# Routed attention and a gated feed-forward block: 32x32 block transposes on VectorE, and a reciprocal by log, exp and a Newton step

## The chip, the cores and the metric

The kernel runs on one core of a Trainium2 chip. The metric is the device time of one execution in microseconds; a comparison takes the median of several executions. The core's engines run side by side, each working through its own list of instructions in order: TensorE (PE; its weight loads are listed as PEld), VectorE (DVE), ScalarE (ACT), GpSimd (POOL), and SyncE (SP), which here only issues transfers. They wait for each other through semaphores. TensorE writes its results to PSUM; everything else lies in SBUF.

## The reference, cut to what matters

There are 4 batches of 8 heads, 768 positions and 64 values per head. Each query and each key is assigned to one of 16 clusters by the largest similarity with a centroid, a query attends only to keys of its own cluster, and the result goes through a feed-forward block with a smooth gate.

```python
def _attn_ref(q, k, v, centroids):            # q, k, v: (4, 8, 768, 64), centroids: (8, 16, 64)
    ...                                       # q_n, k_n, c_n: q, k, centroids divided by their norms
    q_assign = np.argmax(np.einsum('bhsd,hcd->bhsc', q_n, c_n), axis=-1)
    k_assign = np.argmax(np.einsum('bhsd,hcd->bhsc', k_n, c_n), axis=-1)
    mask = q_assign[:, :, :, None] == k_assign[:, :, None, :]
    scores = scale * np.matmul(q, k.transpose(0, 1, 3, 2))
    scores = np.where(mask, scores, -1000000000.0)
    scores = scores - np.max(scores, axis=-1, keepdims=True)
    attn = np.exp(scores)
    attn = attn / (np.sum(attn, axis=-1, keepdims=True) + 1e-09)
    return np.matmul(attn, v)

def _moe_ref(x, w_in, w_out):                 # x: (3072, 512), w_in: (512, 2048), w_out: (2048, 512)
    h = x @ w_in
    sp = np.maximum(h, 0.0) + np.log1p(np.exp(-np.abs(h)))
    g = h * erf(sp)
    return g @ w_out
```

## The kernel before

The 32 heads are worked off as 16 pairs, four pairs to a batch. For each pair the kernel runs `route` (cluster of each query and key, written as masks), `shift` (whether a query finds any key of its cluster, which sets the shift of its scores), then 12 units of `scores` and two of `attend`, one for each half of the queries. `route` and `shift` of the next pair run beside the units of this one, in small portions. The feed-forward block of a batch is a stream of matmuls that is portioned out between the units of the next batch; for the last batch it runs by itself at the end. During the first pairs the kernel also converts the weights, which come as 64-bit floats and are put together from their two 32-bit words by VectorE.

The masks: `qm` and `km` hold, for one head in one half of the partitions, the one-hot cluster (for q multiplied by minus 2 to the 60th, for k inverted), and in the other half a bf16 copy of the other head's q or k. Their product is added to the scores and drives those of foreign clusters far down.

```python
    aq = const.tile([P, HJ, 2, 2, D], BF16, name="aq")
    ak = const.tile([P, HJ, 2, 2, D], BF16, name="ak")
    ...
    def load(p, nm, src, pl):
        ...
        t = pl.tile([P, NJ, 2, D], F32, name="in_" + nm)
        for e in range(2):
            nc.sync.dma_start(out=t[:, :, e], in_=src[b, h0 + e].rearrange("(p j) d -> p j d", p=P))
    ...
    def convert(dst, src):                     # one of 16 pieces of the weights
        ...                                    # load, ACT Square, then seven VectorE steps of 128x1024
        nc.vector.scalar_tensor_tensor(
            out=m, in0=m, scalar=0x40000000, in1=x, op0=ALU.bitwise_xor, op1=ALU.bitwise_and
        )
        ...
    def route(p):
        st = pairs[p]
        for nm in "qk":
            raw = rowp.tile([P, S], F32, name=nm + "T")
            low = rowp.tile([P, 2, S], BF16, name=nm + "m")
            for half in range(2):
                pt = ps_t.tile([P, HJ, P], F32, name="pt", tag="t")
                for jj in range(HJ):
                    nc.tensor.transpose(out=pt[:, jj], in_=st[nm][:, HJ * half + jj]..., identity=ident)
                ...                            # ACT: q copied with the factor D**-0.5, k copied, into raw
                for e in range(2):
                    nc.gpsimd.tensor_copy(out=low[(1 - e) * D : (2 - e) * D, e, ...], in_=raw[...])
                yield
            ...
        load_qk(p + 1)
        psim = ps_t.tile([P, HW], F32, name="psim", tag="t")
        for g in range(4):
            nc.tensor.matmul(psim[2 * C * g : 2 * C * (g + 1)], lhsT=ccT[:, p % HP], ...)
        sims = routep.tile([P, HW], F32, name="sims")
        nc.scalar.copy(out=sims, in_=psim)
        yield
        pt = ps_t.tile([P, HJ, P], F32, name="pt", tag="t")
        for jj in range(HJ):
            nc.tensor.transpose(out=pt[:, jj], in_=sims[:, jj * P : (jj + 1) * P], identity=ident)
        ...                                    # VectorE: mx, the maximum, and its place; GpSimd: times rank;
                                               # VectorE: mr, the maximum of that; aq, ak, the one-hot masks
        for nm, src in (("qm", aq), ("km", ak)):
            pb = ps_t.tile([P, NJ, P], BF16, name="pb", tag="t")
            for j in range(NJ):
                nc.tensor.transpose(out=pb[:, j], in_=src[:, j % HJ, j // HJ]..., identity=identb)
            for e in range(2):
                ...                            # qm: VectorE, times -BIG; km: nc.scalar.copy
            yield

    def shift(p):
        ...
                sm = ps_s.tile([P, 2, 512], F32, name="sm", tag="s")
                ...                            # two matmuls of qm and km
                nc.vector.tensor_reduce(out=nmx[:, t, half], in_=sm[:, :, 0:HW], ...)
        ...

    def scores(u):
        sc = ps_s.tile([P, 2, 512], F32, name="sc", tag="s")
        ...                                    # matmuls of kT and qT, then of km and qm
        nc.scalar.activation(out=pr[:, :, 0:HW], in_=sc[:, :, 0:HW], func=ACT.Exp)
        ...                                    # GpSimd: acc, the sum of pr over the units of a half

    def attend(u0):
        ...                                    # av: matmuls of v and pr
        psum = ps_t.tile([P, HW], F32, name="psum", tag="t")
        for e in range(2):
            nc.tensor.matmul(psum[e * D : (e + 1) * D], lhsT=ones, rhs=st["acc", half][:, e], ...)
        den = routep.tile([P, HW], F32, name="den")
        nc.vector.tensor_scalar_add(out=den, in0=psum, scalar1=S * EPS)
        nc.vector.reciprocal(out=den, in_=den)
        ...                                    # xT = (av + column sum) * den, on VectorE
```

The pool `ps_s` has two buffers, which the tiles sm and sc share; `ps_t` has one, shared by pt, psim, pb, pn and psum. The feed-forward block takes Softplus and Erf from ACT, which has to load another table for these than for Exp.

Of the kernel before, what the change touches and what calls it, by code (L numbers as in the profile page):

```python
# [8 lines left out]
F32 = mybir.dt.float32  # L9
# [8 lines left out]
P = 128  # L18
B, H, S, D = 4, 8, 768, 64
C = 16  # L20
NJ = S // P
HW = S // 2
# [13 lines left out]
SH = 32  # L36
# [6 lines left out]
def kernel(  # L43
# [31 lines left out]
    ones = const.tile([P, D], F32, name="ones")  # L75
# [3 lines left out]
    w_out = const.tile([P, NFT, DM], F32, name="w_out")  # L79

    aq = const.tile([P, HJ, 2, 2, D], BF16, name="aq")
    ak = const.tile([P, HJ, 2, 2, D], BF16, name="ak")
# [9 lines left out]
    def load(p, nm, src, pl):  # L92
        if p >= NPAIR:
            return
        b, h0 = heads(p)
        t = pl.tile([P, NJ, 2, D], F32, name="in_" + nm)
        for e in range(2):
            nc.sync.dma_start(out=t[:, :, e], in_=src[b, h0 + e].rearrange("(p j) d -> p j d", p=P))
        pairs.setdefault(p, {})[nm] = t
# [13 lines left out]
    nc.vector.memset(ones, 1.0)  # L113
    for c in range(C):
        nc.vector.memset(rank[:, c : c + 1], float(C - c))
    nc.vector.memset(ccT, 0.0)
    nc.gpsimd.memset(aq, 0.0)
    nc.gpsimd.memset(ak, 0.0)
    nc.gpsimd.memset(ak[:, :, :, :, SH : SH + 1], 1.0)
# [92 lines left out]
    def route(p):  # L212
        st = pairs[p]
        for nm in "qk":
            raw = rowp.tile([P, S], F32, name=nm + "T")

            low = rowp.tile([P, 2, S], BF16, name=nm + "m")
            for half in range(2):
                pt = ps_t.tile([P, HJ, P], F32, name="pt", tag="t")
                for jj in range(HJ):  # L220
                    nc.tensor.transpose(  # L221
                        out=pt[:, jj], in_=st[nm][:, HJ * half + jj].rearrange("p e d -> p (e d)"),
                        identity=ident,
                    )
                dst = raw[:, half * HW : (half + 1) * HW]
                src = pt.rearrange("p j t -> p (j t)")
                if nm == "q":
                    nc.scalar.mul(out=dst, in_=src, mul=D**-0.5)
                else:
                    nc.scalar.copy(out=dst, in_=src)  # L230
                for e in range(2):
                    nc.gpsimd.tensor_copy(
                        out=low[(1 - e) * D : (2 - e) * D, e, half * HW : (half + 1) * HW],
                        in_=raw[e * D : (e + 1) * D, half * HW : (half + 1) * HW],
                    )
                yield
            st[nm + "T"], st[nm + "m"] = raw, low
            del st[nm]
        load_qk(p + 1)
        psim = ps_t.tile([P, HW], F32, name="psim", tag="t")  # L240
        for g in range(4):
            nc.tensor.matmul(
                psim[2 * C * g : 2 * C * (g + 1)], lhsT=ccT[:, p % HP],
                rhs=st["qk"[g // 2] + "T"][:, (g % 2) * HW : (g % 2 + 1) * HW],
                start=True, stop=True,
            )
        sims = routep.tile([P, HW], F32, name="sims")
        nc.scalar.copy(out=sims, in_=psim)
        yield
        pt = ps_t.tile([P, HJ, P], F32, name="pt", tag="t")  # L250
        for jj in range(HJ):
            nc.tensor.transpose(out=pt[:, jj], in_=sims[:, jj * P : (jj + 1) * P], identity=ident)

        n = HJ * 8
        sim = pt.rearrange("p j (g c) -> p (j g) c", c=C)
        mx = routep.tile([P, n], F32, name="mx")
        nc.vector.reduce_max(out=mx, in_=sim, axis=AX.X)
        oh = sims.rearrange("p (g c) -> p g c", c=C)
        nc.vector.tensor_tensor(
            out=oh, in0=sim, in1=mx.unsqueeze(2).to_broadcast([P, n, C]), op=ALU.is_equal  # L260
        )

        nc.gpsimd.tensor_tensor(
            out=oh, in0=oh, in1=rank.unsqueeze(1).to_broadcast([P, n, C]), op=ALU.mult
        )
        mr = routep.tile([P, n], F32, name="mr")
        nc.vector.reduce_max(out=mr, in_=oh, axis=AX.X)
        for i, (dst, op) in enumerate(((aq, ALU.is_equal), (ak, ALU.not_equal))):
            nc.vector.tensor_tensor(
                out=dst.rearrange("p j h e c -> p j (h e) c")[:, :, :, 0:C],  # L270
                in0=oh.rearrange("p (j x g) c -> p j x g c", j=HJ, x=2)[:, :, i],
                in1=mr.rearrange("p (j x g) -> p j x g", j=HJ, x=2)[:, :, i].unsqueeze(3).to_broadcast(
                    [P, HJ, 4, C]
                ),
                op=op,
            )
        yield

        for nm, src in (("qm", aq), ("km", ak)):
            pb = ps_t.tile([P, NJ, P], BF16, name="pb", tag="t")  # L280
            for j in range(NJ):
                nc.tensor.transpose(  # L282
                    out=pb[:, j], in_=src[:, j % HJ, j // HJ].rearrange("p e c -> p (e c)"),
                    identity=identb,
                )
            for e in range(2):
                r = slice(e * D, (e + 1) * D)
                src = pb[r].rearrange("p j t -> p (j t)")
                if nm == "qm":
                    nc.vector.tensor_scalar_mul(out=st[nm][r, e], in0=src, scalar1=-BIG)  # L290
                else:
# [266 lines left out]
```

## Time and profile before

| What | Value |
|---|---|
| Time, median of 3 executions | 1338.84 us (1338.69 to 1339.38) |
| Span of the profiled execution | 1335.5 us |
| PE busy | 1218.0 us, 91% |
| DVE busy | 640.5 us, 48% |
| ACT busy | 421.0 us, 32% |
| POOL busy | 400.2 us, 30% |
| Packets moved by the DMA engines | 82699, of which 76464 under 512 B |

A profile shows one execution. Busy time is the time in which an engine works on an instruction; a matmul's end is modelled, and matmuls overlap, so a busy PE need not be at its peak. A row of a group gives the line of the kernel, the engine, the operation, the tiles (written, then read), the shapes and the number of instructions, then the busy time in all, the mean duration of one in nanoseconds, and the engine's idle time just before them with what ended it. A single matmul of 32-bit floats leaves two records, a transposition one. Idle time of an engine that does not bound the kernel costs nothing, so the first question to such a page is which engine is full in which part of the span.

### The profile page before, as it was taken

How to read it: one execution, taken by the hardware profiler on the slowest of the kernel's cores; microseconds unless marked ns; L12 is line 12 of the kernel's file. 1: busy time of each engine (PE TensorE's matmuls, PEld its weight loads, DVE VectorE, ACT ScalarE, POOL GpSimd, SP SyncE). 2: the span in 40 equal slices, each digit the busy share in tenths (PEclk: the TensorE clock that was granted, in tenths of full speed). 3: DMA queues.
4: the chain of work that ended last, by engine and by line, in shares of the span. 5: the costliest groups of instructions: out<-in, count | busy, mean ns of one | idle time of the engine just before them, and what ended most of it. 6: DMA issues, size and time to landing. Idle time of an engine off the chain costs nothing.

```text
span 1335.5 us, 13090 instructions
## 1 busy us (share of the span) xinstructions
PE 1218.0 (91%) x5313; PEld 659.5 (49%) x5313; DVE 640.5 (48%) x809; ACT 421.0 (32%) x458; POOL 400.2 (30%) x337
## 2 busy tenths in 40 slices
PE   3676767889999999999999999999999999999998
PEld 1222222346546545444654645545645646575764
DVE  6898999746243525451634534452615413221221
ACT  3232323224416224414423422514424413130321
POOL 3536365452323233423233231522232221000000
PEclk9777889899999999999999999999999999999999
DMA  6213142110101001101001010102000000000000
GB/s 166 87 64 120 42 130 75 24 37 1 36 8 32 12 13 40 36 1 40 12 1 51 2 44 8 36 1 52 1 9 20 1 8 9 8 9 8 8 16 16
DMA packets 82699, 42.90 MB, mean 32 GB/s; under 512 B 76464, under 2 KB 76496, under 8 KB 81616
## 3 DMA queue, kind: packets, MB, share of 16 engines
q1 hardware_dynamic: 79312, 25.31, 7.7%
q0 software_dynamic: 3328, 16.78, 3.7%
q8 instruction: 41, 0.67, 0.2%
q14 instruction: 18, 0.15, 0.0%
HBM read 35.73 MB, written 6.34 MB: 32 GB/s over the span
## 4 chain that ended last, share of the span: by engine, by line
PE 72%; DVE 16%; POOL 4%; ACT 3%; DMA 2%; issue 2%; SPq 0%; POOLq 0%; ACTq 0%; DVEq 0%
PE po L451 24%; PE hp L432 21%; PE av L375 8%; PE sc L345 7%; PE sm L304 4%; DVE nmx L308 3%; DVE den L387 2%; POOL acc L364 2%; PE psum L382 2%; ACT pr L356 2%; PE sc L351 2%; DVE w_x L154 2%; PE pt L221 1%; DVE w_x L157 1%; DVE w_m L148 1%
## 5 line engine op out<-in xcount | busy, mean ns | idle before, releaser
L432 PE MATMUL hp<-xT,w_in 128*128 128x256 f32 x1536 | 379.6, 384 | 0.0
L451 PE MATMUL po<-w_out,g 128*128 128x512 f32 x768 | 370.4, 599 | 2.6 <-DVE g L439 2.0
L364 POOL TENSOR_TENSOR acc<-acc,pr 128x768 f32<-128x768 f32 x128 | 224.2, 1751 | 489.8 <-ACT pr L356 483.0
L432 PEld LDWEIGHTS hp<-xT,w_in 128*128 128x128 f32 x1536 | 284.8, 191 | 99.2 <-issue 67.0
L356 ACT ACTIVATE pr<-sc 128x768 f32<-128x768 f32 x192 | 152.5, 812 | 386.7 <-PE sc L351 384.5
L308 DVE TENSOR_REDUCE nmx<-sm 128x2 f32<-128x768 f32 x192 | 178.6, 953 | 110.0 <-PE sm L304 108.7
L439 DVE COPY g<-hp 128x512 f32<-128x512 f32 x96 | 66.0, 688 | 286.8 <-PE hp L432 286.6
L345 PE MATMUL sc<-qT,kT 64*128 64x384 f32 x768 | 187.1, 549 | 10.3 <-DVE nmx L308 8.4
L451 PEld LDWEIGHTS po<-w_out,g 128*128 128x128 f32 x768 | 139.4, 190 | 107.4 <-issue 90.6
L375 PE MATMUL av<-pr,in_v 128*64 128x386 f32 x768 | 160.1, 511 | 6.6 <-DVE xT L396 6.2
L304 PE MATMUL sm<-km,qm 128*128 128x384 bf16 x384 | 99.1, 347 | 25.8 <-DVE nmx L308 13.7
L345 PEld LDWEIGHTS sc<-qT,kT 64*128 64x128 f32 x768 | 69.2, 199 | 92.5 <-issue 42.1
L360 POOL TENSOR_TENSOR acc<-pr,pr 128x768 f32<-128x768 f32 x32 | 60.6, 1894 | 152.8 <-ACT pr L356 152.6
L375 PEld LDWEIGHTS av<-pr,in_v 128*64 128x64 f32 x768 | 54.8, 139 | 85.4 <-issue 74.8
L415 ACT ACT_TABLE_LOAD x48 | 61.6, 1283 | 105.3 <-DVE g L439 104.5
L417 DVE TENSOR_TENSOR g<-a_s,g 128x512 f32<-128x512 f32 x96 | 66.2, 740 | 50.5 <-ACT a_s L415 50.5
L386 DVE TENSOR_SCALAR den<-psum 128x384 f32<-128x384 f32 x32 | 17.8, 556 | 147.9 <-PE psum L382 147.7
L304 PEld LDWEIGHTS <-qm 128*128 128x128 bf16 x384 | 36.3, 100 | 98.7 <-issue 84.2
L387 DVE RECIPROCAL den<-den 128x384 f32<-128x384 f32 x32 | 81.6, 2550 | 0.7
L351 PE MATMUL sc<-qm,km 64*128 64x384 bf16 x384 | 70.8, 339 | 0.2 <-DMA qm<-line 0.2
L415 ACT ACTIVATE a_s<-g 128x2048 f32<-128x2048 f32 x24 | 45.9, 1911 | 78.4 <-DVE g L439 78.3
L292 ACT COPY km<-pb 64x768 bf16<-64x768 bf16 x32 | 25.4, 793 | 117.8 <-PE pb L282 117.4
(76 smaller groups left out, 720.9 us busy)
## 6 DMA issues: line engine op xcount, KB each, us to landing
raw<-in_moe_w_in_dram POOLq DMA_DIRECT2D x8, 1024.0 KB, 5.7
raw<-in_moe_w_out_dram POOLq DMA_DIRECT2D x8, 1024.0 KB, 5.3
in_q<-in_q_dram SPq DMA_DIRECT2D x32, 192.0 KB
in_k<-in_k_dram SPq DMA_DIRECT2D x32, 192.0 KB
in_v<-in_v_dram SPq DMA_DIRECT2D x32, 192.0 KB
out_dram<-osb SPq DMA_DIRECT2D x24, 256.0 KB
qm<-line SPq DMA_DIRECT2D x32, 1.5 KB
line<-nmT SPq DMA_DIRECT2D x16, 3.0 KB
```

Of the source, the lines that this page charges most:

```text
L304: nc.tensor.matmul(sm[:, e, 0:HW], lhsT=st["qm"][:, e, t * P : (t + 1) * P], rhs=st["km"][:, e, half * HW : (half + 1) * HW], start=True, ...
L308: nc.vector.tensor_reduce(out=nmx[:, t, half], in_=sm[:, :, 0:HW], axis=AX.X, op=ALU.max, negate=True)
L345: nc.tensor.matmul(sc[:, e, 0:HW], lhsT=st["kT"][r, j * P : (j + 1) * P], rhs=st["qT"][r, cols], start=True, stop=False,)
L351: nc.tensor.matmul(sc[:, e, 0:HW], lhsT=st["km"][r, e, j * P : (j + 1) * P], rhs=st["qm"][r, e, cols], start=False, stop=True,)
L356: nc.scalar.activation(out=pr[:, :, 0:HW], in_=sc[:, :, 0:HW], func=ACT.Exp)
L364: nc.gpsimd.tensor_tensor(out=st["acc", half], in0=st["acc", half], in1=pr[:, :, 0:HW], op=ALU.add)
L375: nc.tensor.matmul(av[e * D : (e + 1) * D], lhsT=st["v"][:, j, e], rhs=prs[(u0 + j) % NPT][:, e], start=(j == 0), stop=(j == NJ - 1),)
L387: nc.vector.reciprocal(out=den, in_=den)
L415: nc.scalar.activation(out=s[:, i : i + half], in_=src[:, i : i + half], func=func)
L417: nc.vector.tensor_tensor(out=h[:, i : i + GW], in0=s[:, i : i + GW], in1=h[:, i : i + GW], op=ALU.mult)
L432: nc.tensor.matmul(hp[:, a], lhsT=w_in[:, r, f0 : f0 + P], rhs=xTs[b * HP + r][c], start=(r == 0), stop=(r == HP - 1),)
L451: nc.tensor.matmul(po, lhsT=gs[n][:, ft, tt * P : (tt + 1) * P], rhs=w_out[:, ft], start=(ft == 0), stop=(ft == NFT - 1),)
```

## The change

TensorE no longer turns anything in `route`. VectorE has an operation that transposes each 32x32 block of a tile by itself. The loads of q and k are laid out so that this is enough: a partition group of 32 receives, for 24 blocks of positions, 32 of the 64 values of a head, and after the block transposition the tile has the values on the partitions and the positions in order. The similarities are turned in the same way straight from PSUM, and the one-hot masks as one tile of bf16. With that the layout of the tiles in between changes: `qm` and `km` become two fixed pairs of tiles that are cleared once, the row that holds the shift is set to zero for each pair anew, the clusters' rank carries the factor for the keys, and a small vector `own` picks the head and its sign. The factor D**-0.5 moves from the copy of q into the Exp of the scores. The purpose is to take work from TensorE, ACT and PSUM, at the price of loads in runs of 32 floats (128 B) for q and k.

The reciprocal of the sum is made differently as well: ACT computes exp(-ln(sum)), and two VectorE operations make one Newton step of it. The sum now comes out of its matmul with a minus sign, which saves a step. v and the output are addressed with position = 128 j + p in place of 6 p + j, in runs of the same size as before.

```diff
-        t = pl.tile([P, NJ, 2, D], F32, name="in_" + nm)
-        for e in range(2):
-            nc.sync.dma_start(out=t[:, :, e], in_=src[b, h0 + e].rearrange("(p j) d -> p j d", p=P))
+        if nm == "v":
 ...
+            t = pl.tile([P, NB, Q], F32, name="in_" + nm)
+            for e in range(2):
+                for g in range(D // Q):
+                    nc.sync.dma_start(
+                        out=t[e * D + g * Q : e * D + (g + 1) * Q],
+                        in_=src[b, h0 + e, :, g * Q : (g + 1) * Q].rearrange("(n t) d -> t n d", t=Q),
+                    )
 ...
     def route(p):
         st = pairs[p]
+        low = lows[p % 2]
         for nm in "qk":
             raw = rowp.tile([P, S], F32, name=nm + "T")
-            low = rowp.tile([P, 2, S], BF16, name=nm + "m")
-            for half in range(2):
-                pt = ps_t.tile([P, HJ, P], F32, name="pt", tag="t")
-                for jj in range(HJ):
-                    nc.tensor.transpose(
 ...
-                if nm == "q":
-                    nc.scalar.mul(out=dst, in_=src, mul=D**-0.5)
-                else:
-                    nc.scalar.copy(out=dst, in_=src)
 ...
+            nc.vector.transpose(out=raw, in_=st.pop(nm).rearrange("p n t -> p (n t)"))
+            for e in range(2):
+                nc.gpsimd.tensor_copy(out=low[nm][(1 - e) * D : (2 - e) * D, e], in_=raw[e * D : (e + 1) * D])
+            st[nm + "T"], st[nm + "m"] = raw, low[nm]
+            yield
+        for e in range(2):
+            nc.gpsimd.memset(low["q"][e * D + SH : e * D + SH + 1, e], 0.0)
         load_qk(p + 1)
 ...
         sims = routep.tile([P, HW], F32, name="sims")
-        nc.scalar.copy(out=sims, in_=psim)
-        yield
-        pt = ps_t.tile([P, HJ, P], F32, name="pt", tag="t")
-        for jj in range(HJ):
-            nc.tensor.transpose(out=pt[:, jj], in_=sims[:, jj * P : (jj + 1) * P], identity=ident)
+        nc.vector.transpose(out=sims, in_=psim)
 ...
+        hot = routep.tile([P, HW], BF16, name="hot")
+        for r, op in ((slice(0, D), ALU.is_equal), (slice(D, P), ALU.subtract)):
             nc.vector.tensor_tensor(
 ...
+                out=hot[r].rearrange("p (g c) -> p g c", c=C), in0=sim[r],
+                in1=mr[r].unsqueeze(2).to_broadcast([D, n, C]), op=op,
+            )
+        hotT = routep.tile([P, HW], BF16, name="hotT")
+        nc.vector.transpose(out=hotT, in_=hot)
+        for half in range(2):
+            cols = slice(half * HW, (half + 1) * HW)
+            for e in range(2):
+                r = slice(e * D, e * D + Q)
+                g = slice(half * Q, (half + 1) * Q)
+                nc.vector.tensor_scalar_mul(out=low["q"][r, e, cols], in0=hotT[g], scalar1=own[g, e : e + 1])
+                g = slice(D + half * Q, D + (half + 1) * Q)
+                nc.scalar.copy(out=low["k"][r, e, cols], in_=hotT[g])
         yield
-        for nm, src in (("qm", aq), ("km", ak)):
-            pb = ps_t.tile([P, NJ, P], BF16, name="pb", tag="t")
-            for j in range(NJ):
-                nc.tensor.transpose(
 ...
-        nc.scalar.activation(out=pr[:, :, 0:HW], in_=sc[:, :, 0:HW], func=ACT.Exp)
+        nc.scalar.activation(out=pr[:, :, 0:HW], in_=sc[:, :, 0:HW], func=ACT.Exp, scale=D**-0.5)
 ...
+        inv = routep.tile([P, HW], F32, name="inv")
         den = routep.tile([P, HW], F32, name="den")
-        nc.vector.tensor_scalar_add(out=den, in0=psum, scalar1=S * EPS)
-        nc.vector.reciprocal(out=den, in_=den)
+        nc.scalar.activation(out=inv, in_=psum, func=ACT.Ln, bias=alleps, scale=-1.0)
+        nc.scalar.activation(out=inv, in_=inv, func=ACT.Exp, scale=-1.0)
+        nc.vector.scalar_tensor_tensor(
+            out=den, in0=psum, scalar=S * EPS, in1=inv, op0=ALU.subtract, op1=ALU.mult
+        )
+        nc.vector.scalar_tensor_tensor(
+            out=den, in0=den, scalar=2.0, in1=inv, op0=ALU.add, op1=ALU.mult
+        )
```

## The prediction, made before the changed kernel had run

> **What bounds the kernel now.** I read the busy shares first, then the 40 slices, then busy time by stage, then the chain of waits and who waits for whom inside each stage.
>
> ```profile
> PE 1218.0 (91%) x5313; PEld 659.5 (49%) x5313; DVE 640.5 (48%) x809; ACT 421.0 (32%) x458; POOL 400.2 (30%) x337
> PE   3676767889999999999999999999999999999998
> DVE  6898999746243525451634534452615413221221
> ```
>
> TensorE (PE) is busy for 91% of the span, VectorE (DVE) for 48%, but the slices show two stages. For the first eight or nine slices (33 us each) DVE is at 7 to 9 tenths and PE at 6 or 7; from slice ten on PE is at 9 throughout. Busy time by stage, from windows of the trace (columns: length, PE, PEld, DVE, ACT, POOL, granted clock, DMA share, GB/s):
>
> ```profile
> 0.00:300.00 300.00, 207.50 (x909) 81.83 (x910) 248.12 (x286) 84.20 (x116) 146.68 (x130) 0.86 0.29 83
> 300.00:1140.00 840.00, 819.15 (x3780) 459.16 (x3779) 352.02 (x462) 295.07 (x316) 253.57 (x207) 1.00 0.07 19
> 1140.00:1336.00 196.00, 191.37 (x629) 118.56 (x627) 40.41 (x63) 41.70 (x27) 0.00 (x0) 1.00 0.03 11
> ```
>
> So **early** (0 to 300 us) DVE is the bound: it converts the weights and serves the first pairs, and between 10 and 250 us it is busy for 220 of 240. **Late** (300 to 1140) PE is the bound with 819 of 840 us; DVE and ACT have half their time free. In the **tail** (from 1140) only the feed-forward part of the last batch is left on PE, and the change does not touch it. Removed work therefore counts by engine and stage: PE work late, DVE work early.
>
> The rows that the change takes away (busy, mean ns, idle before, who ended it):
>
> ```profile
> L387 DVE RECIPROCAL den<-den 128x384 f32<-128x384 f32 x32 | 81.6, 2550 | 0.7
> L386 DVE TENSOR_SCALAR den<-psum 128x384 f32<-128x384 f32 x32 | 17.8, 556 | 147.9 <-PE psum L382 147.7
> L290 DVE TENSOR_SCALAR qm<-pb 64x768 bf16<-64x768 bf16 x32 | 17.7, 554 | 4.3 <-PE pb L282 4.1
> L292 ACT COPY km<-pb 64x768 bf16<-64x768 bf16 x32 | 25.4, 793 | 117.8 <-PE pb L282 117.4
> ```
>
> A matmul's busy time overlaps the next one's, so I take what a transposition costs PE from the time between the starts of a group and of the next in the late timeline (start, length):
>
> ```profile
> 554.16 0.55 PE L221 MATMUL pt<-ident,in_q 128*128 128x128 f32 x3
> 554.64 2.16 PE L375 MATMUL av<-pr,in_v 128*64 128x386 f32 x10
> ...
> 566.11 0.49 PE L252 MATMUL pt<-ident,sims 128*128 128x128 f32 x3
> 566.44 3.62 PE L432 MATMUL hp<-xT,w_in 128*128 128x256 f32 x16
> 571.32 0.51 PE L282 MATMUL pb<-identb,aq 128*128 128x128 bf16 x6 [1.26 <-DVE aq L269]
> 571.66 1.51 PE L432 MATMUL hp<-xT,w_in 128*128 128x256 f32 x6
> ```
>
> Three q transpositions cost 0.48 us, three of the similarities 0.33, six of a mask 0.34. The bracket shows a second cost: PE stood 1.26 us because the mask was not ready. Of PE's 21 us of idle time in the late stage, this wait is over half:
>
> ```profile
> PE pb L282 <- DVE aq L269: 12.1, 9, 2.4
> PE sc L345 <- DVE nmx L308: 2.8, 1, 2.8
> ```
>
> **What the Trainium skill says.** "VectorE: DVE Perf Modes", section "The three transpose paths": the VectorE transpose makes 32x32 blocks only and takes 311 ns for 128x128 bf16. No run here has one yet. The trace's one-source DVE op without a fast mode, the reduce of 384 elements from SBUF (mr, 552 ns), has about the same fixed part, at some 1.05 ns per element (xT: 483 ns for 256 elements, 348 for 128). "SBUF — State Buffer", section "Who interferes with whom": a DVE op with two SBUF inputs, or in a two-port mode, and a GpSimd op that reads SBUF block each other. The trace agrees: the same 1024-element w_m step of L148 takes 1.22 us alone and 2.58 us beside POOL's acc. "ScalarE: Activation LUTs", section "Table sets", puts exp and ln into one set, so that they would need one load. It gives some 2.7 us for a switch; the trace has 1.283 us for each ACT_TABLE_LOAD, and I use that. "DMA: Bandwidth & Descriptors", section "Why small descriptors are slow (HBM only)", gives every packet an overhead that does not shrink with it; the trace of before has only larger packets in these loads, so what 128 B cost is taken up below.
>
> **The change, part by part.**
>
> *PE.* Per pair: 12 transpositions of q and k (4 x 0.48 = 1.92), 3 of the similarities (0.33), 12 of the masks (0.68) go: 2.93 us. Ten of the 16 routings fall into the late stage (120 of 192 records of L221 lie there): **-29 us** on the engine that bounds. With the masks off PE, the 12.1 us wait goes too, but the chain mask to qm to sm stays and can make PE stand at sm; I credit 7. The reciprocal blocks DVE for 2.55 us, and the nmx behind it then holds both buffers of ps_s: at 543.0 to 546.4 us PE waits 2.8 us for this. I credit 3. Waits: **-10 us**.
>
> *ACT.* Per pair it loses q, k and similarity copies (2 x 0.490 + 2 x 0.475 + 0.476 = 2.4 us) and gains two Ln and two Exp of 384 elements (4 x 0.49 = 2.0); the mask copies go from 2 x 0.79 to four of 32x384 (about 0.5 each): even, some 32% busy. But in the instruction list of the built program, once Softplus and Erf have begun, Ln and Exp no longer share a table: a load stands before 24 of the Ln and before 17 of the Exp behind them. Loads go from 73 to 115, 42 x 1.283 = 54 us of ACT. ACT has room for that (295 of 840 late), but each block (load, Ln, load, Exp: 3.5 us) sits in front of the exponentials that free the two ps_s buffers. Between psum and the next need of a buffer PE has two score tiles (about 2 us) and one slot of feed-forward (1.4 us), so it runs dry by perhaps half a microsecond per block. 24 x 0.5: **+12 us**, my least certain term.
>
> *DVE early.* Six routings and eight halves fall there. Removed: 8 x (2.55 + 0.556) + 6 x (2 x 0.554 + 0.355 + 0.350) = 35.7 us. Added per routing: two transposes of 768 (0.955 each, from 552 ns plus 384 x 1.05), two of 384 (0.55 each), two hot (0.55 each, as L259's 553), four qm of 32x384 (estimate 0.25): 5.1 us; per half two scalar_tensor_tensor (0.61 from PSUM, 0.55): 1.16. 6 x 5.1 + 8 x 1.16 = 39.9 us. So DVE is not relieved: **+4 us**. Most of what comes in has two SBUF inputs or a fast mode, while what goes (reciprocal, PSUM reads) did not compete with POOL. The competing ops (is_equal, hot, qm, the second Newton step) come to 20 us; the weight steps run at about 1.35 times their time alone, so I add 0.35 x 20 = 7. Shorter ways through PE and ACT give perhaps 5 back from the 20 us in which DVE idles between 10 and 250.
>
> *Transfers.* q and k come in runs of 32 floats: 6144 packets of 128 B per pair for 3072 of 256 B. In the first 16 us the hardware queue moved 8784 packets at 65.2% of 16 engines, 19 ns each. If a 128 B packet costs nearly as much, the first q and k take about 7 us instead of 3.6, beside the first weights, and eight DMA issues of 0.65 us instead of four. k landed at about 11.2 us; I expect 13 to 14: **+2 us** early. Later a pair has some 70 us to load: hidden.
>
> Early: 4 + 7 - 5 + 2 = +8. Late: -29 - 10 + 12 = -27. Sum -19: 1339 - 19 = 1320 us.
>
> **Rivals.** (1) *ACT's tables give nothing to PE.* For: the kernel already has 48 loads with Softplus and Erf in blocks of 6 us, and late PE waits for ACT by name only 2.3 us. Then the +12 is nearly 0, and I get 1305 to 1308. Against: some blocks now follow Erf directly, and the reserve of two buffers is small. (2) *ACT becomes the wait that replaces the others.* With 1 to 1.5 us per block, +24 to +36, the gain is gone: 1332 to 1344. ACT still shows under 50% busy then, which is why the share would not tell it. (3) *The early stage decides.* If the f32 transpose costs two cycles per element, six routings add 6 x 2.7 = 16 us of DVE, where DVE is the bound, and the result is about 1336. Against: the page's 311 ns fit one element per cycle. (4) *Transfers stop being hidden.* If 128 B runs cost far more than a packet now, DVE, which takes its work in order, stands at its transpose and the weight conversion behind it. 29% DMA share early leaves a reserve of three.
>
> **Range and chances.** The PE term is solid to within 4 us; ACT (0 to 30), waits (0 to 15) and the early stage (-5 to +20) carry the spread, about 17 us together. 2% faster would be 1312, half a spread below my estimate: one in three. 2% slower is 1366 and needs two rivals together. 1320 us, range 1297 to 1342; faster 0.33, within 2% 0.59, slower 0.08.
>
> **What the new profile would show.** PE: busy time down by about 45 (29 late, the rest early), no pb or pt rows, no wait for aq. ACT: 42 more loads, busy near 475; if PE waits on pr by over 20 us late, rival 2 holds, if by under 5, rival 1. DVE: transposes of 768 near 0.95 us (else rival 3), DVE early as full as before, PE's dense stage starting 5 to 10 us later. The first sm should start near 27 us as now; a start after 32 means the loads cost more than I say. The prediction is wrong if PE's late windows stay at 97 to 99% with no shorter span, or if early DVE idles at a transpose for in_q or in_k.

## The result, and the profile after

| | before | after |
|---|---|---|
| Time, median of 4 executions | 1338.76 us (1335.38 to 1339.38) | 1354.39 us (1353.67 to 1356.27) |
| Span of the profiled execution | 1335.5 us | 1352.7 us |
| Packets moved | 82699 | 132875 |

The ratio is 1.0124, with a 95% interval of 1.0104 to 1.0144: the change made the kernel slower by 1.2%, 34 us from the predicted 1320 us and outside the range of 1297 to 1342.

The busy shares, the slices of PE and DVE and the granted clock on the page of the changed kernel:

```profile
PE 1191.9 (88%) x4881; PEld 630.4 (47%) x4881; DVE 655.2 (48%) x924; ACT 476.7 (35%) x516; POOL 416.9 (31%) x310
PE   1686676579999899889999989899999999999998
DVE  5989999974443525441634443542625302221221
PEclk9978777879899999989999989989999999999999
```

And busy time by stage, with the columns as in the prediction (length, PE, PEld, DVE, ACT, POOL, granted clock, DMA share, GB/s):

```profile
0.00:300.00 300.00, 190.81 (x725) 65.04 (x726) 261.94 (x337) 82.03 (x116) 147.32 (x122) 0.84 0.31 83
300.00:1140.00 840.00, 792.82 (x3438) 437.36 (x3437) 348.62 (x517) 341.91 (x364) 262.85 (x185) 0.97 0.09 19
```

PE does 432 matmuls less, but after slice nine it is no longer at 9 throughout: 792.8 us busy in the 840 of the late stage, for 819.2 before. And its clock in that stage is 0.97, for 1.00 before. PE, which bounds this stage, now stands. What it stands for, in the late stage (total us, times, longest):

```profile
PE sm L306 <- ACT pr L358: 30.8, 11, 10.0
PE po L461 <- DVE g L449: 7.8, 3, 4.1
PE hp L442 <- DVE g L449: 2.8, 2, 1.4
```

The wait for the mask (12.1 us) is gone. In its place stand 30.8 us at the matmul of the shift, in few and long stops, for a score buffer that ACT's exponential frees. Before, that wait was short in all and in each:

```profile
PE sm L304 <- ACT pr L356: 2.1, 12, 0.4
```

To compare runs I cut every span at two matmuls: the sum (psum) of the fourth pair's second half ends the early stage, and the last psum ends the late one. "Half clock" is the sum, over windows of 20 us from 300 to 1160 us, of length times one minus the granted clock. "PE idle" is the same stretch of 860 us less PE's busy time; the two overlap where PE stands at half clock. The time is a median; the four columns on the right are read from the one profiled execution of each kernel, which for e1 was 3.8 us below the median and for e2 5.7 above it, so a few us between two rows show nothing by themselves.

| Kernel | Time, us | Ratio to before (95%) | Early ends at | Late | Half clock | PE idle |
|---|---|---|---|---|---|---|
| before | 1338.8 | | 289.5 | 846.5 | 3.6 | 20.8 |
| after | 1354.4 | 1.0124 (1.0104 to 1.0144) | 293.2 | 860.0 | 25.8 | 47.5 |
| e1_noload | 1329.6 | 0.9932 (0.9909 to 0.9956) | 289.2 | 835.3 | 17.2 | 28.4 |
| e2_km_dve | 1350.6 | 1.0092 (1.0061 to 1.0124) | 305.5 | 849.6 | 17.2 | 44.1 |
| e3_recip | 1331.6 | 0.9950 (0.9933 to 0.9968) | 294.5 | 835.4 | 15.4 | 32.1 |
| e4_ln_before | 1340.9 | 1.0032 (1.0023 to 1.0042) | 290.6 | 849.1 | 0.0 | 25.3 |
| e5_rank_dve | 1337.1 | 0.9998 (0.9988 to 1.0009) | 289.5 | 845.9 | 14.0 | 37.3 |
| e6_start | 1359.9 | 1.0162 (1.0140 to 1.0185) | 296.1 | 864.4 | 29.0 | 53.7 |
| e7_recip_rank | 1328.7 | 0.9938 (0.9916 to 0.9959) | 297.3 | 829.8 | 12.2 | 25.9 |
| e8_recip_rank_start | 1329.0 | 0.9936 (0.9914 to 0.9959) | 297.9 | 829.6 | 10.6 | 27.2 |
| e9_split | 1324.2 | 0.9899 (0.9876 to 0.9923) | 291.7 | 832.1 | 14.0 | 24.2 |
| e10_rank_noload | 1310.4 | 0.9800 (0.9769 to 0.9832) | 290.4 | 818.4 | 5.2 | 18.8 |
| e12_setload | 1326.4 | 0.9919 (0.9905 to 0.9932) | 290.8 | 833.4 | 14.4 | 27.8 |
| e13_rank_setload | 1314.6 | 0.9827 (0.9813 to 0.9840) | 292.1 | 822.3 | 8.0 | 21.0 |

The loss of 17.2 us of span is 3.7 early, 13.5 late and nothing in the tail (199.5 us in both). So the question is why the late stage, from which TensorE work was taken, is longer.

One of the long stops, from the timeline of the changed kernel (start, length, engine, instruction; the bracket is the idle time before and what ended it):

```profile
565.58 1.09 DVE L267 TENSOR_TENSOR sims<-sims,mx 128x384 f32<-128x384 f32 x1
566.31 1.91 POOL L246 CAST qm<-qT 64x768 bf16<-64x768 f32 x2
568.29 1.71 POOL L246 CAST km<-kT 64x768 bf16<-64x768 f32 x2
570.08 1.82 POOL L362 TENSOR_TENSOR acc<-pr,pr 128x768 f32<-128x768 f32 x1
571.85 1.00 POOL L272 TENSOR_TENSOR sims<-sims,rank 128x384 f32<-128x384 f32 x1
572.88 0.55 DVE L276 TENSOR_REDUCE mr<-sims 128x24 f32<-128x384 f32 x1 [6.22 <-POOL sims L272]
...
575.23 2.07 ACT L294 COPY km<-hotT 32x384 bf16<-32x384 bf16 x4 [10.84 <-DVE hotT L286]
577.32 1.28 ACT L390 ACT_TABLE_LOAD   x1
578.61 0.58 ACT L390 ACTIVATE inv<-psum,alleps 128x384 f32<-128x384 f32 x1
579.21 1.28 ACT L358 ACT_TABLE_LOAD   x1
580.50 0.81 ACT L358 ACTIVATE pr<-sc 128x768 f32<-128x768 f32 x1
581.46 0.80 PE L306 MATMUL sm<-km,qm 128*128 128x384 bf16 x2 [10.04 <-ACT pr L358]
```

Read it from below. PE stood 10.04 us until ACT's exponential freed a score buffer. ACT had been idle for 10.84 us and then did, in the order of its list, four mask copies (2.07 us), a table load, the logarithm and another load before that exponential, whose scores had long been there. The copies were late because the mask was late: VectorE was ready for the rank step at 566.67 us, but GpSimd (POOL), which has it, first ran casts and a sum and came to it at 571.85. Such a delay is not the rule: of the ten pairs routed in the late stage, the rank step starts 5.2 us after VectorE was ready in two, and within 0.1 us in the other eight. The second of the two makes the second longest stop, 7.88 us:

```profile
873.86 0.55 DVE L276 TENSOR_REDUCE mr<-sims 128x24 f32<-128x384 f32 x1 [6.23 <-POOL sims L272]
882.44 0.80 PE L306 MATMUL sm<-km,qm 128*128 128x384 bf16 x2 [7.88 <-ACT pr L358]
```

Two suspects follow: the **loads** between the sum and the exponentials, and the **rank step** in GpSimd's queue, with the mask copies ahead in ACT's. The experiments take them away one at a time and together.

### The profile page after: what moved, and what is told of

Read it like the earlier page. It is cut to its first block, busy times and chain, and to the rows that moved or that the text cites. A ratio compares the mean times of both kernels' runs of the same rounds, so it can differ in the third digit from the quotient of the medians.

```text
span 1352.7 us, 12507 instructions
## 1 busy us (share of the span) xinstructions
PE 1191.9 (88%) x4881; PEld 630.4 (47%) x4881; DVE 655.2 (48%) x924; ACT 476.7 (35%) x516; POOL 416.9 (31%) x310
## 2 busy tenths in 40 slices
DMA packets 132875, 42.88 MB, mean 32 GB/s; under 512 B 126640, under 2 KB 126672, under 8 KB 131792
## 4 chain that ended last, share of the span: by engine, by line
PE 67%; DVE 16%; ACT 8%; issue 4%; POOL 4%; DMA 1%; POOLq 0%; DVEq 0%; ACTq 0%
PE po L461 24%; PE hp L442 21%; PE sc L347 7%; PE av L377 6%; PE sm L306 4%; DVE nmx L310 2%; PE sc L353 1%; DVE g L427 1%; ACT L390 1%; ACT pr L358 1%; PE psum L384 1%; ACT km L294 1%; POOL acc L366 1%; DVE hot L281 1%; DVE w_m L175 1%
## 5 line engine op out<-in xcount | busy, mean ns | idle before, releaser
L442 PE MATMUL hp<-xT,w_in 128*128 128x256 f32 x1536 | 383.9, 387 | 2.8 <-DVE g L449 2.8
L461 PE MATMUL po<-w_out,g 128*128 128x512 f32 x768 | 374.4, 607 | 10.4 <-DVE g L449 7.8
L366 POOL TENSOR_TENSOR acc<-acc,pr 128x768 f32<-128x768 f32 x128 | 231.3, 1807 | 447.0 <-ACT pr L358 442.0
L442 PEld LDWEIGHTS hp<-xT,w_in 128*128 128x128 f32 x1536 | 290.3, 193 | 118.7 <-issue 80.7
L347 PE MATMUL sc<-qT,kT 64*128 64x384 f32 x768 | 193.8, 561 | 22.2 <-DVE nmx L310 16.3
L306 PE MATMUL sm<-km,qm 128*128 128x384 bf16 x384 | 105.1, 360 | 84.6 <-ACT pr L358 33.8
L377 PE MATMUL av<-pr,in_v 128*64 128x386 f32 x768 | 159.2, 522 | 22.2 <-DVE xT L406 11.2
L392 DVE SCALAR_TENSOR_TENSOR den<-psum,inv 128x384 f32<-128x384 f32 x32 | 17.8, 556 | 151.0 <-ACT inv L391 150.9
L294 ACT COPY km<-hotT 32x384 bf16<-32x384 bf16 x64 | 32.5, 508 | 89.7 <-DVE hotT L286 88.9
L165 ACT ACTIVATE w_x<-raw 128x1024 f32<-128x1024 f32 x16 | 18.2, 1138 | 78.8 <-DMA raw<-in_moe_w_in_dram 36.7
```

Source lines behind the costliest of these rows:

```text
L306: nc.tensor.matmul(sm[:, e, 0:HW], lhsT=st["qm"][:, e, t * P : (t + 1) * P], rhs=st["km"][:, e, half * HW : (half + 1) * HW], start=True, ...
L347: nc.tensor.matmul(sc[:, e, 0:HW], lhsT=st["kT"][r, j * P : (j + 1) * P], rhs=st["qT"][r, cols], start=True, stop=False,)
L366: nc.gpsimd.tensor_tensor(out=st["acc", half], in0=st["acc", half], in1=pr[:, :, 0:HW], op=ALU.add)
L377: nc.tensor.matmul(av[e * D : (e + 1) * D], lhsT=st["v"][:, j, e], rhs=prs[(u0 + j) % NPT][:, e], start=(j == 0), stop=(j == NJ - 1),)
L442: nc.tensor.matmul(hp[:, a], lhsT=w_in[:, r, f0 : f0 + P], rhs=xTs[b * HP + r][c], start=(r == 0), stop=(r == HP - 1),)
L461: nc.tensor.matmul(po, lhsT=gs[n][:, ft, tt * P : (tt + 1) * P], rhs=w_out[:, ft], start=(ft == 0), stop=(ft == NFT - 1),)
```

## The experiments

**Loads.** An exponential in place of the logarithm leaves the logarithm out, so the output is not the reference's. All else in the instruction lists stays, and the loads fall from 115 to 73.

```diff
-        nc.scalar.activation(out=inv, in_=psum, func=ACT.Ln, bias=alleps, scale=-1.0)
+        nc.scalar.activation(out=inv, in_=psum, func=ACT.Exp, bias=alleps, scale=1.0)
```

> The changed kernel with Exp in the place of Ln (the log and so the reciprocal are left out; the result is not the reference's). The instruction lists of all engines stay the same but for ACT's table loads: 73 in place of 115. Theory Q (ACT's queue: the four mask copies stand in its list ahead of the exponentials that free ps_s, and wait for a mask that hangs behind GpSimd's casts): the loads are only the smaller part of each stop, PE still stands at sm for ACT over 15 us late, time 1340 to 1350. Theory L (the table loads themselves): 54 us of ACT go, PE's waits for pr fall under 5 us as before, time 1318 to 1332.

Measured: 1329.57 us; the late stage is 24.7 us shorter than with the loads, and the waits for pr fall from 30.8 to 17.1 us:

```profile
PE sm L306 <- ACT pr L358: 17.1, 3, 8.5
```

The time is that of theory L, but the waits do not fall under 5 us as it had it: three stops are left, up to 8.5 us long. The 42 loads are 54 us of ACT's time, and PE's late stage lost nearly half of that.

**Mask copies of k off ACT.**

```diff
-                nc.scalar.copy(out=low["k"][r, e, cols], in_=hotT[g])
+                nc.vector.tensor_copy(out=low["k"][r, e, cols], in_=hotT[g])
```

> The changed kernel with the four mask copies of k on VectorE beside those of q, the table loads kept. Theory Q: nothing on ACT waits for the mask any more, the stops of 10.0 and 7.9 us at sm vanish and with them the dips of PE's clock; PE's late waits for pr under 10 us, time 1318 to 1332. Theory L: 41 loads before Ln and Exp are still there, time within 6 us of the changed kernel, 1348 to 1360.

Measured: 1350.64 us (1344.47 to 1356.3). Late it gains 10.4 us, early it loses 12.3, where VectorE is the bound and gets four copies more for each pair; both figures are of the profiled execution, the slowest of the six. In the late stage PE now stands 13.7 us at sm for VectorE's km, up to 8.0 at a time. So the exponentials no longer queue behind the copies, but the mask itself still comes late. The place of the copies is at most a part of the cost.

**The two halves of the change alone.** First the block transpositions with the exact reciprocal of before (the column of minus ones becomes ones):

```diff
-        nc.scalar.activation(out=inv, in_=psum, func=ACT.Ln, bias=alleps, scale=-1.0)
-        nc.scalar.activation(out=inv, in_=inv, func=ACT.Exp, scale=-1.0)
 ... (and the two scalar_tensor_tensor)
+        nc.vector.tensor_scalar_add(out=den, in0=psum, scalar1=S * EPS)
+        nc.vector.reciprocal(out=den, in_=den)
```

> The changed kernel with the exact reciprocal on VectorE back (add and reciprocal, 3.1 us per half), the block transposes kept. Theory L: loads back to 73, PE late waits gone, 1318 to 1332. Theory Q: the mask copies still stand ahead of the exponentials, only the loads between them go; 1338 to 1352, and early about 7 us are added since VectorE is the bound there.

Then the kernel before with the logarithm, exponential and Newton step alone (its column of ones becomes minus ones, and the first Newton step is written over psum):

```diff
-        nc.vector.tensor_scalar_add(out=den, in0=psum, scalar1=S * EPS)
-        nc.vector.reciprocal(out=den, in_=den)
+        nc.scalar.activation(out=den, in_=psum, func=ACT.Ln, bias=alleps, scale=-1.0)
+        nc.scalar.activation(out=den, in_=den, func=ACT.Exp, scale=-1.0)
 ... (and the two scalar_tensor_tensor)
```

> The kernel before with the reciprocal by log, exp and a Newton step alone (its first step written over psum), all transpositions on TensorE. Theory L: 42 more loads cost here what they cost in the changed kernel, over 20 us: 1358 to 1372. Theory Q: ACT's mask copies follow PE's pb and do not hang behind GpSimd, so the loads cost little and the reciprocal's VectorE time early is saved: 1330 to 1346.

Measured: a ratio to the kernel before of 0.9950 for the transpositions alone, 1.0032 for the reciprocal alone, 1.0124 for both. Effects that did not touch would give 0.998. The reciprocal adds 2.6 us to the late stage of the kernel before (846.5 to 849.1), but 24.6 us to that of the transposed one (835.4 to 860.0), with 42 more loads each time. What differs in the traces is where a load falls. ACT's waits for the sum in the late stage, of the kernel before with the new reciprocal:

```profile
ACT den L388 <- PE psum L384: 106.8, 19, 11.6
```

and of the changed kernel:

```profile
ACT L390 <- PE psum L384: 40.6, 8, 7.7
ACT inv L390 <- PE psum L384: 36.1, 6, 10.0
```

The stage has 23 sums with a logarithm behind them. In the first kernel the wait belongs to the logarithm 19 times: its load (the line without a tile) ran ahead of the wait, while ACT had nothing to do. In the second it belongs to the logarithm only 6 times. In 8 cases the load itself stands behind the wait; why was not found. In the other 9, in 8 of them straight from the mask copies, ACT begins the load within about half a us of the sum's end or, in three as in the stop above, 3.6 to 8.8 us after it. So 17 times a load of 1.28 us stands between the sum and the exponentials; the second load of a block stands there in both kernels. An estimate from these counts: 17 x 1.28 is 21.8 us, and the reciprocal costs 22.0 us more here than there (24.6 less 2.6). No run moved these 17 loads alone, so it is not shown that their place is the whole difference.

**Rank step from GpSimd to VectorE.**

```diff
-        nc.gpsimd.tensor_tensor(
+        nc.vector.tensor_tensor(
             out=sim, in0=sim, in1=rank.unsqueeze(1).to_broadcast([P, n, C]), op=ALU.mult
```

> The changed kernel with the multiplication by rank on VectorE in the place of GpSimd, loads kept. Theory M (the second half of the stops is the mask itself, which comes late because its rank step queues on GpSimd behind casts and acc): the two long stops at sm fall from 10.0 and 7.9 us to under 5, late stage 8 to 12 us shorter; VectorE's early work grows by 6 times 0.55 us and what competition with GpSimd adds; time 1342 to 1350. Theory L alone: the stops stay within 2 us of what they were, 1352 to 1358.

Measured: 1337.10 us, under the range that I expected, since the early stage became shorter (by 3.7 us) and not longer. The late stage is 14.1 us shorter than the changed kernel's. The two stops of 10.0 and 7.9 us fall to 5.8 and 3.3:

```profile
570.15 0.80 PE L306 MATMUL sm<-km,qm 128*128 128x384 bf16 x2 [5.80 <-ACT pr L358]
```

The step is also shorter on VectorE (a median of 0.56 us, for 1.00 on GpSimd in the stop above); no run separates that from the queue. With both suspects away (the logarithm is left out again):

> The changed kernel with rank on VectorE and Exp in the place of Ln (the log and so the reciprocal left out; not the reference's result). Loads cost 25 us and the late rank step 17 us each by itself; if they are separate costs, 1312 to 1316; if they are the same stops counted twice, 1322 to 1330.

Measured: 1310.35 us, late stage 818.4, PE at 821 of 840 us, clock 0.99, waits for pr 6.6 us:

```profile
300.00:1140.00 840.00, 821.25 (x3602) 454.15 (x3601) 369.23 (x542) 302.30 (x334) 257.73 (x177) 0.99 0.09 19
PE sm L306 <- ACT pr L358: 6.6, 3, 3.1
```

The two costs add, to within 3 us. The loads cost 24.7 us with the rank on GpSimd (860.0 less 835.3) and 27.5 without (845.9 less 818.4); the rank step costs 14.1 with the loads and 16.9 without. The medians of the whole kernel say the same: 24.8 and 26.8 us for the loads, 17.3 and 19.2 for the rank step.

**The start.** The changed kernel clears its mask tiles on GpSimd ahead of the issue of the first weights: the issue starts at 14.56 us (2.83 before), VectorE stands 9.0 us for them, and the first sm comes at 32.38 us (27.21 before). Here the first weights go first, and the clearing behind:

```diff
-    for t in lows:
-        nc.gpsimd.memset(t["q"], 0.0)
 ...
+    convert(*w_steps.pop(0))
+    for t in lows:
+        nc.gpsimd.memset(t["q"], 0.0)
```

> The changed kernel with the first weight piece asked for and converted ahead of the first routing, and the clearing of the mask tiles behind its load. If the head's loss is GpSimd's clearing in front of the weight transfer (first weights at 21.7 us, VectorE idle 9 us), the dense stage starts 5 to 10 us earlier and the time is 1344 to 1350. If the 128 B transfers set the head, it stays within 3 us.

Measured: 1359.93 us, slower by 5.5 us, which neither of my two cases had. The first sm came later still, at 35.87 us, and between 40 and 300 us VectorE was as full as in the changed kernel (235.8 and 235.6 of 260 us). So it does not shorten the early stage to let the weights go first. Nor does VectorE's sum of work alone set its length: with the rank step on VectorE (e5) it is busy for 264.7 us up to the end of the stage, for 257.6 in the changed kernel, and the stage ends 3.7 us sooner. The late stage lost 4.4 us more, all in the waits for pr (35.2 us for 30.8); why these grew was not found.

**Exact reciprocal and rank on VectorE, without and with the new start.** The edits are those above.

> The changed kernel with the exact reciprocal on VectorE (no added table loads) and the rank step on VectorE. Loads and late mask both gone: stops at sm under 3 us each, 1316 to 1326. If the mask's lateness has another cause, it stays where the exact reciprocal alone was, 1328 to 1334.

> As before this, and the first weight piece ahead of the first routing: 4 to 8 us below the run with exact reciprocal and rank on VectorE, so 1310 to 1322, faster than both kernels.

Measured: 1328.68 and 1329.01 us, both above what I expected. The late stage does as asked (829.8 us, stops at sm for pr of 2.6 us at most), but the reciprocal's 2.55 us a half come back on VectorE early, where the stage ends at 297 us. The start again gives nothing.

**A reciprocal for each stage.** The logarithm only for the first four pairs, where no load is needed, and the exact reciprocal for the other twelve; rank on VectorE.

```diff
+        if p < HP:
             nc.scalar.activation(out=inv, in_=psum, func=ACT.Ln, bias=alleps, scale=-1.0)
 ...
+        else:
+            nc.vector.tensor_scalar(
+                out=den, in0=psum, scalar1=-1.0, scalar2=S * EPS, op0=ALU.mult, op1=ALU.add
+            )
+            nc.vector.reciprocal(out=den, in_=den)
```

> The changed kernel with rank on VectorE, and the reciprocal by log, exp and a Newton step only for the first four pairs, where Ln and Exp share the loaded table and VectorE is the bound; the exact reciprocal (3.1 us of VectorE) for the other twelve, where VectorE has room. No table loads beyond the 73. If the parts add up as the runs so far say, the first stage ends as in the run with rank on VectorE (289 us) and the late stage takes what it took with the exact reciprocal and rank on VectorE (830 us): 1316 to 1323. If VectorE's reciprocal early did not matter, it stays at 1326 to 1331.

Measured: 1324.19 us, 1.0% under the kernel before, with nothing left out, and just above the 1316 to 1323 that I expected.

**The clock by itself.** In the stop above, PE's granted clock by windows of 3 us (length, PE busy, clock, DMA share, GB/s):

```profile
570.00:573.00 3.00, 1.42 (x8) 1.00 0.42 93
576.00:579.00 3.00, 0.00 (x0) 0.50 0.00 0
582.00:585.00 3.00, 3.00 (x9) 0.50 0.02 5
588.00:591.00 3.00, 3.00 (x17) 1.00 0.00 0
```

The clock is halved while PE stands, and stays so after it works again. The same six records of the feed-forward block take nearly twice as long at half clock:

```profile
582.05 2.77 PE L442 MATMUL hp<-xT,w_in 128*128 128x256 f32 x6
589.13 1.46 PE L442 MATMUL hp<-xT,w_in 128*128 128x256 f32 x6
```

To measure this alone, a kernel that computes nothing of the reference runs bursts of 48 equal matmuls of 512 columns of 32-bit floats; between bursts a chain on VectorE makes PE wait, from 1.2 to 9.2 us:

```diff
+    for gap in GAPS:
+        po = ps.tile([P, DM], F32, name="po")
+        for i in range(BURST):
+            nc.tensor.matmul(po, lhsT=w, rhs=x, start=(i == 0), stop=(i == BURST - 1))
+        nc.vector.tensor_copy(out=y, in_=po)
+        for _ in range(gap - 1):
+            nc.vector.tensor_tensor(out=y, in0=y, in1=y, op=ALU.max)
```

> Not the kernel: 14 bursts of 48 f32 matmuls of 512 columns (about 20 us each at full clock), with waits of about 1.5 to 8 us between them made of VectorE steps, twice over; everything else is left out. If a stop of TensorE costs its clock as well, the bursts behind the longer waits begin at half clock for 3 to 7 us and are longer by half of that, and those behind waits under about 3 us are not. If the clock in the traces is not of the waits' making, all bursts take the same time.

From its timeline, of one execution (start, length of the burst, and in the bracket the stop before it):

```profile
45.91 41.47 PE L48 MATMUL po<-x,w 128*128 128x512 f32 x96 [1.24 <-DVE x L52]
89.35 43.16 PE L48 MATMUL po<-x,w 128*128 128x512 f32 x96 [1.97 <-DVE x L52]
135.21 44.53 PE L48 MATMUL po<-x,w 128*128 128x512 f32 x96 [2.70 <-DVE x L52]
282.49 44.27 PE L48 MATMUL po<-x,w 128*128 128x512 f32 x96 [6.33 <-DVE x L52]
```

Behind a stop of 1.24 us the burst takes 41.47 us, both times that it comes. Behind every stop from 1.97 us on it takes 42.85 to 44.53, so 1.4 to 3.1 us more, with no clear growth for a longer stop. That stops of 1.97 and 2.70 us cost it too is more than I expected. One stop of 3 us thus costs PE 3 us and about 2 again. Short waits need not: the kernel before with the new reciprocal (e4) has 25.3 us of idle time in the stretch, with 1.64 us as the longest stop, and no half clock at all.

**The set of tables, chosen by hand.** What was still open was whether the loads or the logarithm itself cost the 25 us, since e1 left out both. Here the kernel asks, behind each Erf, for the set that has logarithm and exponential together; the line is already used once at the kernel's start. Nothing is left out of the computation.

```diff
                 nc.scalar.activation(out=s[:, i : i + half], in_=src[:, i : i + half], func=func)
+                if func == ACT.Erf:
+                    tc.keep_in_program_order(nc.scalar.preload_act_table_set("natural_log_exp_and_others"))
```

> The changed kernel, with one load of the table set that holds both the logarithm and the exponential put by hand behind each of the 24 Erf instructions. In the instruction list 2 loads stand before Ln (24 before), none before the Exp behind it (17 before), 11 before the exponentials of the scores (24 before); with the 24 placed ones there are 37 for 65. The order of instructions on the engines shifts a little with it. Nothing of the computation is left out. Theory (the loads that stand between the sum and the exponentials of the scores cost 25 us): about 1331 us, as with the log left out (1329.6), and PE waits for pr for under 20 us late. Rival (the logarithm itself, two more ACT steps and the Newton step cost it, not the loads): 1345 or more.

The same with the rank step on VectorE:

> The same with the rank multiply on VectorE as well. Theory (the two costs, loads and rank step, add, and both can be taken away without leaving anything out): 1310 to 1316 us, as with the log left out and the rank on VectorE (1310.35), 2% under the kernel before; PE over 97% busy from 300 to 1140 us. Rival (the gain with the log left out came from the shorter work or other values): 1322 or more.

Measured: 1326.41 and 1314.61 us. The first is at the level of e1, so it is the loads and not the logarithm: the late stage has 64 for 98. (Some of them the kernel before had too: 11 in place of 24 stand before the exponentials of the scores.) The second takes 1.7% off the kernel before, the best version here that computes all of the reference. PE's wait for pr and its late stage there:

```profile
PE sm L306 <- ACT pr L358: 6.8, 5, 3.1
```

```profile
300.00:1140.00 840.00, 818.97 (x3591) 452.61 (x3590) 369.58 (x544) 312.89 (x342) 258.60 (x178) 0.99 0.09 19
```

PE is at 97.5% again, as before the change, with the transpositions gone; ACT has 342 instructions there for 364.

## Why the prediction was wrong, step by step

Late I had predicted -27 us and measured +13.5, which is 40.5 apart. Taking the steps in the order e10, e5, changed kernel, the waits account for 22 us of that, the loads for 15.5 and PE's work for 3.

**PE's work: right.** The prediction took 29 us off the late stage. With both new costs away (e10) it is 28.1 us shorter (846.5 to 818.4), some 2 of them by less idle time, which leaves 26.

**ACT's loads: the mechanism right, the size wrong.** The first step that failed is "24 x 0.5: +12 us". Measured, the loads cost 24.7 us, or 27.5 with the rank moved: 1.1 to 1.2 us for each of the 23 blocks in the stage (24.7 or 27.5 over 23). That is the prediction's second rival. I had set the block of 3.5 us against a reserve of 3.4 and counted a stop as its own length. From e10 to e5 the loads add 18.5 us of idle time (37.3 less 18.8) and 8.8 us of half clock (14.0 less 5.2), together 27.3 of the 27.5; so by this count about a third of their cost is the clock. The late mask copies do not explain the size: with the mask earlier, the loads cost no less. How much of the idle time comes from the place of the loads, and how much from the smaller reserve of a PE with less work to do, was not measured. And e12 shows that the cost was never one of logarithm and exponential as such: two instructions' choice of table set made it. The Trainium skill, "ScalarE: Activation LUTs", section "Table sets: the hidden batching unit", has both in one set, for which one load is enough. The trace agrees only where that set is asked for: 2 loads at the logarithm and none behind it in e12, for 24 and 17.

**The waits: wrong in sign.** The second step that failed is "Waits: -10 us". The mask wait did go, but in e10 PE's idle time is 18.8 us for 20.8 before, so the credit was 2. And the chain from the mask to sm, which the prediction had named and thought to be covered by crediting 7 of 12.1 us, cost far more, by a step that it had not named: the rank step in GpSimd's queue. That step and the casts stood on GpSimd before as well; but then the similarities went through an ACT copy and PE first, and now they can reach GpSimd while it still has casts, and 32 clearings of 758 ns that are new. In the kernel before none of the ten late rank steps starts more than 1.5 us after VectorE was ready, in the changed one two start 5.2 us after. And the copies that need the result stand ahead of the exponentials in ACT's list. Putting the rank step on VectorE shows what its place costs: 14.1 to 16.9 us (e5, e10).

**The late sum** is then 846.5, less 28.1 for the work and the small credit (818.4, e10), plus 27.5 for loads (845.9, e5), plus 14.1 for the rank step: 860.0. It closes because each step is the difference of two runs; the check is that taking the costs away in the other order gives nearly the same sizes, 24.7 and 16.9.

**The clock: left out.** Neither of the failed steps had it. The Trainium skill, "TensorE: Matmul & The Clock Gate", section "Part 1: The HAM clock gate (the "warmup" mystery)", says that an idle window of some 3.4 us halves the clock and a busy one restores it; I didn't use it, since the kernel before lost only 3.6 us to it. The trace shows the two levels, 0.5 and 1.0. From before to after, the half clock grows by 22.2 us and the idle time by 26.7; they overlap and cannot simply be added. From e5 to the changed kernel, for the rank step alone, they grow by 11.8 and 10.2 us and the stage by only 14.1: the rank step costs mainly two long stops, in and behind which PE is at half clock.

**VectorE early: direction right, the size in part by luck.** Predicted +8 us, measured +3.7. Up to the end of the stage VectorE is busy for 257.6 us, for 239.9 before: 17.7 more, where I had 11 (4 and 7). But its idle time there fell by 14 us (49.6 to 35.6), where I had given back 5. The two errors nearly cancel. The transposition is as estimated: 384 elements more take 0.39 us more (0.974 less 0.582), so about 1.02 ns each, and rival 3, with twice that, is out. (Its 2.7 us for a routing was too much by its own figures: 1920 elements of 32-bit floats at 1.05 ns more are 2.0.) The groups of the changed kernel (busy, mean ns, idle before):

```profile
L244 DVE STREAM_TRANSPOSE qT<-in_q 128x768 f32<-128x768 f32 x16 | 15.6, 974 | 41.6 <-PE sc L347 41.5
L262 DVE STREAM_TRANSPOSE sims<-psim 128x384 f32<-128x384 f32 x16 | 9.3, 582 | 39.7 <-PE psim L255 39.2
L395 DVE SCALAR_TENSOR_TENSOR den<-den,inv 128x384 f32<-128x384 f32 x32 | 27.0, 842 | 0.8
```

0.974 and 0.582 us for the estimated 0.955 and 0.55. The second Newton step is at 842 ns for an estimated 550. Of the 32, 23 take 0.56 us or less, as estimated. The other nine all begin while a sum (acc) runs on GpSimd, and end about 0.41 us after it; none that began before its acc is slow. So this is the competition with GpSimd that I had allowed for. One of the nine:

```profile
158.65 2.16 POOL L366 TENSOR_TENSOR acc<-acc,pr 128x768 f32<-128x768 f32 x1 [0.46 <-ACT pr L358]
159.19 2.03 DVE L395 SCALAR_TENSOR_TENSOR den<-den,inv 128x384 f32<-128x384 f32 x1
```

**Transfers: wrong in mechanism, without effect.** I expected k at 13 to 14 us; VectorE turned it at 9.54. The first sm came at 32.38 and not near 27, but for GpSimd's clearing ahead of the first weights, not for the loads of q and k; in e6 and e8, where the weights go first, the stage ends no sooner. VectorE never idled for in_q or in_k.

**The signs named.** PE waits on pr by over 20 us late: this was said to mean rival 2, and did. ACT busy near 475 with 42 more loads: 476.7. PE's busy time fell by 26 and not 45, partly because matmuls at half clock take longer; read alone, it would have hidden that the work was gone.

## What to carry to other kernels

When work is taken from the engine that bounds, ask what the instructions that replace it stand behind in the in-order queues of the others. Here 42 table loads came with a net cost of 2.6 us in a kernel where about half of them stood in front of a wait, and of 25 in one where most stood behind it; choose the set by hand where two functions share one. And read the longest stop, not only the sum of stops: here a few stops of several us cost PE its clock as well, and many short ones did not.

## What the runs showed of the hardware that I had not expected

- A stop of 1.97 us was enough to halve PE's clock afterwards, one of 1.24 us was not (e11, each twice). That is less than the idle window quoted above; here the measurement decides, for this pattern of work. In e11 the clock's record changes only after whole multiples of 3.413 us, and the half clock lasts one to three of them.
- Small packets cost less than expected: in the first 10 us the changed kernel moved 6416 packets of 128 B at 50.9% of 16 engines, so 12.7 ns each (0.509 x 16 x 10 us / 6416), for 19 ns before with mostly 256 B. Beside the first weights, in e6, it is 12.8 ns (6041 packets at 48.3%).
